# The last two tail-row results of an attention + MoE kernel: one 128-partition store each in place of two 64-partition stores

## The chip, the cores and the metric

The kernel runs on one core of a Trainium2 chip. The metric is device time in microseconds (us) of one execution, taken as the median of several runs. A profile is one more execution of the same program, recorded by the hardware; times inside it count from the first instruction of the span.

In what follows PE is the matrix engine, DVE the vector engine, ACT the scalar engine, POOL the GpSimd engine and SP the engine that does nothing but issue transfers and wait. A "q" behind a name (SPq, ACTq) is the instruction queue of that engine. All transfers run on the core's 16 DMA engines. Those that SP issues stand in the profile as queue q1, those that ACT issues as queue q10. A transfer is cut into packets, here one packet for each contiguous piece of memory, and closes with small 4-byte packets that raise its semaphore.

## The reference

Eight batches of eight heads of 576 tokens go through a linear attention with random features. The result is laid out as 4608 tokens x 512 and multiplied through a gated pair of weights:

```python
q_p, k_p = (phi(q_s), phi(k_s))
kv = np.einsum('bhsm,bhsd->bhmd', k_p, v)
z = np.sum(k_p, axis=2)
num = np.einsum('bhsm,bhmd->bhsd', q_p, kv)
den = np.einsum('bhsm,bhm->bhs', q_p, z)[..., None] + 1e-06
attn = num / den
x = attn.transpose(0, 2, 1, 3).reshape(B * S, H * D)      # 4608 x 512
a, b = x @ w_a, x @ w_b                                   # 4608 x 1536 each
return (a * b) @ w_out                                    # 4608 x 512, float32
```

## The kernel before

**Tiles of rows.** The 4608 rows of x are worked through in nine tiles of 512. Tiles 0 to 7 are the first 512 rows (`SM`) of each of the eight batches. The ninth tile, `b == B`, gathers the 64 tail rows (`TL`, rows 512 to 575) of all eight batches: 8 x 64 = 512 rows. It is the last work of the program. In it 128 partitions hold two batches: partitions 0 to 63 the tail rows of one batch (`j = 0`), partitions 64 to 127 those of the next (`j = 1`). A half `th` of the tile is four batches, which are two such groups of 128 rows, called t = 0 and 1 (or "parts").

**Order.** Every operation is recorded in a graph; a planner with costs, due times and tables of shifts lays out one order for all engines, and the program is emitted in that order. Each engine runs its own queue in that order and waits on semaphores. A transfer is an instruction in the queue of SP or of ACT, waits there for its data, is issued, and the engine goes on while the data moves.

**The output product.** The last two tiles use a scheme of seven block products (class `Out7`), so a result block of 256 rows x 256 columns is a sum of several PSUM banks and buffers in SBUF. Four buffers `oc` of 128 partitions x 2 parts x 256 columns hold the four blocks of the tile (half `th` of the rows, half `dh` of the columns). In the last tile, `second(q, dh)` (line 1267) makes the last product of a block, adds it to `oc` (`add`, line 1211, on DVE) and stores the block (`store`, line 1219). Three blocks are finished whole: one DVE addition of 128 x 512 and then the store. The fourth, (1, 1), the last of the program, is finished in two parts: for each t, the three matmuls of that part, a DVE addition of 128 x 256 (line 1213), and a store of that part.

**The stores of the last tile.** `rows` (line 1227) is the view of the output with axes j (2), r (64 rows of a batch), t and c (256 columns, 1 KB in a row). For each block or part, `store` issues two transfers: j = 0 on SP's queue, j = 1 on ACT's queue. So in the last tile there are three pairs of whole stores (64 rows x 2 parts x 1 KB, 128 KB each) and two pairs of part stores (64 rows x 1 KB, 64 KB each): ten transfers, five for each queue. Behind them SP waits for all transfers to land, and a closing sequence of all engines ends the program.

**Two other transfers that the prediction counts.** `zdr<-zx` writes 8 rows of 32 numbers (8 packets of 128 bytes). `xtd<-xts` writes 128 partitions x 4 pieces of 64 numbers (512 packets of 256 bytes). No other transfer has data packets under 512 bytes.

Of the kernel before, what the change touches and what calls it, by code (L numbers as in the profile page):

```python
# [18 lines left out]
P = 128  # L19
# [3 lines left out]
E, FF = H * D, 1536  # L23
# [3 lines left out]
HM = SM // 2  # L27
NFP = NF // 2
B1 = 2
TL = S - SM  # L30
# [352 lines left out]
def tile_attention_moe(ctx: ExitStack, tc: tile.TileContext, kqt, kqtt, kqn, kqnt, vx, omst, idn, wab, wout, out):  # L383
    nc = tc.nc
# [11 lines left out]
    g = Graph()  # L396
# [45 lines left out]
    def dma(dst, src):  # L442
        return lambda e: nc.sync.dma_start(dst(), src())
# [63 lines left out]
    for kind, i, ws in units:  # L507
# [27 lines left out]
        if kind == "o":  # L535
# [3 lines left out]
                 nbytes=P * 2 * E * 4)  # L539
# [630 lines left out]
    class Out7:  # L1170
# [48 lines left out]
        def store(self, o, th, dh, part=None):  # L1219

            b, cols = self.b, slice(HM * dh, HM * dh + HM)
            if b < B:
                r0 = b * S + HM * th
                g.op({"SP": 330}, dma(lambda: out[r0:r0 + HM, cols].rearrange("(t p) c -> p t c", p=P), lambda: o.ap[:]), r=[(o, None)], prio=-5,
                     nbytes=P * E * 4)
                return
            rows = out.rearrange("(n s) c -> n s c", s=S)[4 * th:4 * th + 4, SM:S, cols].rearrange("(t j) r c -> j r t c", j=2)
            tt = slice(0, 2) if part is None else slice(part, part + 1)
            for j, (eng, queue) in enumerate((("SP", nc.sync), ("ACT", nc.scalar))):
                g.op({eng: 330}, lambda e, j=j, queue=queue: queue.dma_start(rows[j][:, tt], o.ap[TL * j:TL * j + TL, tt]),  # L1230
                     r=[(o, part)], prio=-5, nbytes=TL * E * (4 if part is None else 2))

        def items(self, i, C, ghl, Sg, wo, ot):

# [288 lines left out]
    for b in range(B + 1):  # L1523
        if b < B1:
            moe_block(b)
        else:
            if b == B:

                for hp in range(NHP):
# [3 lines left out]
                         prio=-20, nbytes=P * SM * 4, deps=[steps[NF * (B - 1) + CFG["XL"][0]]])  # L1533
# [88 lines left out]
```

## Time and profile before

| | us |
|---|---|
| median of 3 runs | 1020.82 |
| lowest and highest of them | 1020.35, 1022.02 |
| the profiled execution's own time | 1018.96 |
| its span, first to last instruction | 1017.2 |
| PE busy in the span | 1006.6 (99%) |
| granted TensorE clock, mean of the span | 0.999 |

The profiled execution is 1.76 us longer than its span, and 1.86 us shorter than the median of the runs. The page gives busy times by engine, the span in 40 slices, the DMA queues and the chain of work that ended last; queries of the trace give rows by line, by window of time and by queue. The rows below were read from them. A window "A:B" is in us from the span's start.

### The profile page before, as it was taken

To read this page: it belongs to the slowest core of one execution; us is meant where nothing else is said; L and a number is where in the kernel's file an instruction comes from. 1 tells how busy PE (TensorE), PEld (TensorE's weight loads), DVE (VectorE), ACT (ScalarE), POOL (GpSimd) and SP (SyncE) were. 2 spreads that over 40 slices of the span, in tenths; PEclk is the share of its full clock that TensorE was granted. 3 is DMA by queue.
4 is the path that set the end of the run, shared out by engine and by line. 5 is a ranking of instruction groups with operands and counts; after the bars stand their busy time and mean duration, and the time that the engine had idled before them with its cause. 6 is when DMAs were issued, how large, how long until landed. Compare 5 with 4: busy or idle time off the path is not lost.

```text
span 1017.2 us, 27457 instructions
## 1 busy us (share of the span) xinstructions
PE 1006.6 (99%) x10538; PEld 890.0 (87%) x10538; DVE 873.1 (86%) x2162; ACT 574.6 (56%) x1584; POOL 110.7 (11%) x157
## 2 busy tenths in 40 slices
PE   9999999999999999999999999999999999999998
PEld 7777777777888999889988988988998999999997
DVE  7999999899997989877896889888887578999776
ACT  7998797667755647655663656575554024232221
POOL 0131212100111111110210111111110000000000
PEclk9999999999999999999999999999999999999999
DMA  9777887898999999999899889988887889999991
GB/s 356 289 268 256 284 258 223 302 337 306 307 332 383 308 311 303 330 321 312 269 317 357 285 288 328 335 286 294 279 300 256 295 290 347 315 354 337 374 328 44
DMA packets 123428, 306.76 MB, mean 302 GB/s; under 512 B 17952, under 2 KB 41248, under 8 KB 123296
## 3 DMA queue, kind: packets, MB, share of 16 engines
q1 hardware_dynamic: 122416, 304.34, 86.6%
q8 instruction: 83, 1.36, 0.6%
q10 hardware_dynamic: 880, 0.66, 0.2%
q14 instruction: 49, 0.40, 0.1%
HBM read 249.60 MB, written 55.34 MB: 300 GB/s over the span
## 4 chain that ended last, share of the span: by engine, by line
PE 92%; DVE 5%; DMA 1%; ACT 1%; issue 1%; SPq 0%; DVEq 0%; ACTq 0%
PE p L1418 39%; PE o L1137 23%; PE pb L1327 6%; PE pa L1327 6%; PE o_P L1206 5%; PE pkv L918 3%; PE ppk L641 3%; PE p L641 2%; PE p L990 2%; DMA X<-in_kqt_dram 1%; PE p L1206 1%; DVE sm L667 1%; PE ppq L641 1%; DVE raw L490 1%; PE pm L990 1%
## 5 line engine op out<-in xcount | busy, mean ns | idle before, releaser
L1428 DVE TENSOR_TENSOR c<-p,c 128x512 f32<-128x512 f32 (+1 forms) x336 | 208.0, 619 | 63.7 <-PE p L1418 60.7
L1137 PE MATMUL o<-wo,ghl 128*128 128x512 f32 x1008 | 255.9, 395 | 0.2 <-issue 0.2
L1137 PEld LDWEIGHTS o<-wo,ghl 128*128 128x128 f32 x1008 | 180.9, 188 | 38.5 <-issue 5.4
L1418 PE MATMUL p<-x,w 128*128 128x256 f32 x1008 | 136.2, 281 | 0.3 <-DVE c L1428 0.2
L1418 PEld LDWEIGHTS p<-x,w 128*128 128x128 f32 x1008 | 130.6, 189 | 6.6 <-DVE c L1428 0.9
L1418 PE MATMUL p<-Sa,t 128*128 128x256 f32 x1008 | 128.5, 276 | 0.0
L1418 PEld LDWEIGHTS p<-Sa,t 128*128 128x128 f32 x1008 | 121.0, 188 | 0.1
L432 ACT COPY c<-p 128x256 f32<-128x256 f32 x84 | 31.0, 369 | 115.1 <-PE p L1418 103.9
L948 ACT ACTIVATE hq<-hq,dn 128x128 f32<-128x128 f32 x224 | 69.7, 391 | 29.5 <-DVE dn L944 29.2
L865 POOL TENSOR_TENSOR z<-hk 128x256 f32<-128x256 f32 x28 | 25.2, 899 | 523.8 <-ACT hk L680 402.3
L1418 PE MATMUL p<-x,t 128*128 128x256 f32 x504 | 72.0, 278 | 0.8 <-DVE oc L1216 0.8
L938 DVE CUSTOM_DVE_ANT_0 zero<-hq,zb 128x128 bf16<-128x128 f32 x224 | 68.2, 304 | 4.1
L1418 PE MATMUL p<-Sb,bq 128*128 128x256 f32 x504 | 71.3, 277 | 0.0
L1418 PE MATMUL p<-Sb,t 128*128 128x256 f32 x504 | 71.0, 276 | 0.0
L680 ACT ACTIVATE hq<-hq,sm 128x128 f32<-128x128 f32 x196 | 64.7, 391 | 7.5 <-DVE sm L675 7.4
L1418 PEld LDWEIGHTS p<-x,t 128*128 128x128 f32 x504 | 64.8, 188 | 2.3 <-DVE oc L1216 1.0
L680 ACT ACTIVATE hk<-hk,sm 128x128 f32<-128x128 f32 x188 | 61.2, 391 | 8.2 <-DVE sm L675 8.1
L1418 PEld LDWEIGHTS p<-Sb,bq 128*128 128x128 f32 x504 | 63.9, 188 | 0.1
L1418 PEld LDWEIGHTS p<-Sb,t 128*128 128x128 f32 x504 | 63.6, 188 | 0.0
L432 ACT CAST ghl<-c 128x512 fp32r<-128x512 f32 (+1 forms) x60 | 32.8, 566 | 44.2 <-PE o L1137 25.8
L440 DVE TENSOR_TENSOR ghl<-c,ghl 128x512 fp32r<-128x512 f32 (+1 forms) x86 | 54.0, 641 | 4.2 <-ACT ghl L432 3.5
L1478 DVE TENSOR_TENSOR c<-c,c 128x512 f32<-128x512 f32 x82 | 55.5, 711 | 0.7
(245 smaller groups left out, 1898.4 us busy)
## 6 DMA issues: line engine op xcount, KB each, us to landing
t<-td SPq DMA_DIRECT2D x168, 512.0 KB
wo<-wod SPq DMA_DIRECT2D x96, 512.0 KB
bq<-bd SPq DMA_DIRECT2D x84, 256.0 KB
qdr<-qd SPq DMA_DIRECT2D x112, 144.0 KB
hq<-qdr SPq DMA_DIRECT2D x28, 576.0 KB
X<-in_kqt_dram SPq DMA_DIRECT2D x30, 512.0 KB
td<-ts SPq DMA_DIRECT2D x24, 512.0 KB
v<-in_vx_dram SPq DMA_DIRECT2D x28, 288.0 KB
```

Of the source, the lines that this page charges most:

```text
L432: nc.scalar.copy(o(), i())
L440: return lambda e: ENG[e].tensor_tensor(o(), i(), f(hi()), op=ALU.subtract)
L641: nc.tensor.matmul(flat4(pps[w])[half, c * M:c * M + M], x()[rows, c * P:c * P + P][:, half], om.ap[rows], start=True, stop=True)
L680: g.op({"ACT": 393 if b >= B1 or not own else 359}, lambda e, c=c, w=w, to=to, at=at: nc.scalar.activation(to.ap[:, at + c], src[w](c), AF ...
L938: g.op({"DVE": 302}, lambda e, c=c, qc=qc: nc.vector.tensor_tensor_reduce(out=junk.ap[:], in0=qc(), in1=zb.ap[:], scale=1.0, scalar=0.0, o ...
L948: g.op({"ACT": 392}, lambda e, c=c, src=src: nc.scalar.activation(hq.ap[:, c], src(), AF.Copy, scale=dn.ap[:, c:c + 1]), r=[sd, (dn, None) ...
L1137: nc.tensor.matmul(po.ap[:], ghl.ap[:, gi, t * P:(t + 1) * P], wo.ap[:, wi], start=(n == 0 and i == 0), stop=(n == NF - 1 and i == 2))
L1206: nc.tensor.matmul(pb.ap[:, t], A[0](ai)[:, t * P:(t + 1) * P], W[0](wi), start=begin and t == j == 0, stop=stop and t == 1 and j == 2)
L1327: nc.tensor.matmul(pb.ap[:], wt.ap[:, wi, c], xs[c].at(xi), start=(c == 0 and i == 0), stop=(c == NC4 - 1 and i == 2))
L1418: nc.tensor.matmul(pb.ap[:, half], wcol(wi, c), xc(xi, c), start=n == 0, stop=n == 5)
L1428: g.op({"DVE": dve(n)}, lambda e: nc.vector.tensor_tensor(c4.ap[:, o], pb.ap[:, half], y(), op=ALU.add), r=[*((pb, k) for k in range(half. ...
L1478: g.op({"DVE": dve(SM)}, lambda e, v=v, C=C: nc.vector.tensor_tensor(v(C[1]), v(C[1]), v(C[0]), op=ALU.mult), r=part, w=part[2:], prio=-10)
```

## The change

For a part store (`part is not None`) the loop over the two 64-partition halves is gone. One transfer takes all 128 partitions of the part: part 0 is issued on SP's queue and part 1 on ACT's queue. The whole stores are unchanged. Bytes, order of work and buffers are unchanged.

```diff
             rows = out.rearrange("(n s) c -> n s c", s=S)[4 * th:4 * th + 4, SM:S, cols].rearrange("(t j) r c -> j r t c", j=2)
             tt = slice(0, 2) if part is None else slice(part, part + 1)
-            for j, (eng, queue) in enumerate((("SP", nc.sync), ("ACT", nc.scalar))):
+            queues = ("SP", nc.sync), ("ACT", nc.scalar)
+            if part is not None:
+                eng, queue = queues[part]
+                g.op({eng: 330}, lambda e: queue.dma_start(rows[:, :, tt], o.ap[:, tt]),
+                     r=[(o, part)], prio=-5, nbytes=P * HM * 4)
+                return
+            for j, (eng, queue) in enumerate(queues):
                 g.op({eng: 330}, lambda e, j=j, queue=queue: queue.dma_start(rows[j][:, tt], o.ap[TL * j:TL * j + TL, tt]),
-                     r=[(o, part)], prio=-5, nbytes=TL * E * (4 if part is None else 2))
+                     r=[(o, part)], prio=-5, nbytes=TL * E * 4)
```

The order on PE, DVE and POOL is the same in both kernels. The end of SP's queue, with the dimensions of each transfer's pattern in the output behind its name (`oc_0` to `oc_3` are the four blocks, the branch is the end of the program):

```order
-L1230 DMA out_dram<-oc_0_13599 64x2x256
-L1230 DMA out_dram<-oc_1_14444 64x2x256
-L1230 DMA out_dram<-oc_2_14452 64x2x256
-L1230 DMA out_dram<-oc_3_14467 64x256 x2
-L1617 UNCONDITIONAL_BRANCH
+L1236 DMA out_dram<-oc_0_13599 64x2x256
+L1236 DMA out_dram<-oc_1_14444 64x2x256
+L1236 DMA out_dram<-oc_2_14452 64x2x256
+L1232 DMA out_dram<-oc_3_14467 2x64x256
+L1623 UNCONDITIONAL_BRANCH
```

The last two transfers of 64 x 256 have become one of 2 x 64 x 256. The end of ACT's queue, of the kernel before and of the changed one:

```order
L432 CAST ghl_10_14392<-c_51_14355 128x256
L1230 DMA out_dram<-oc_0_13599 64x2x256
L1230 DMA out_dram<-oc_1_14444 64x2x256
L1230 DMA out_dram<-oc_2_14452 64x2x256
L1230 DMA out_dram<-oc_3_14467 64x256 x2
L1617 UNCONDITIONAL_BRANCH
```

```order
L432 CAST ghl_10_14392<-c_51_14355 128x256
L1236 DMA out_dram<-oc_0_13599 64x2x256
L1236 DMA out_dram<-oc_1_14444 64x2x256
L1236 DMA out_dram<-oc_2_14452 64x2x256
L1232 DMA out_dram<-oc_3_14467 2x64x256
L1623 UNCONDITIONAL_BRANCH
```

ACT's queue changes in the same way. The leading dimension of the pattern in the output is the pair j (2), since the two 64-row halves belong to two batches that lie 576 rows apart; on the SBUF side the pattern leads with 128 partitions.

## Rows read from the trace of the kernel before

**Rows 1.** The page: busy time of each engine, share of the span, instructions.

```profile
PE 1006.6 (99%) x10538; PEld 890.0 (87%) x10538; DVE 873.1 (86%) x2162; ACT 574.6 (56%) x1584; POOL 110.7 (11%) x157
```

**Rows 2.** Chain of work that ended last, from 1010: start us, us, what.

```profile
1009.95 1.56 PE o_P L1206 x13
1011.51 0.73 PE p L1206 x6
1012.24 0.02 issue
1012.26 0.42 DVE oc L1213
1012.69 0.33 DVEq L1617
```

**Rows 3.** Timeline: last DVE additions; issues on SP and ACT: start us, us.

```profile
1012.60 0.41 DVE L1213 TENSOR_TENSOR oc<-p,oc 128x256 f32<-128x256 f32 x1
1010.11 0.68 SPq L1230 DMA_DIRECT2D out_dram<-oc  x1
...
1012.26 0.60 SPq L1230 DMA_DIRECT2D out_dram<-oc  x1
1012.27 0.63 ACTq L1230 DMA_DIRECT2D out_dram<-oc  x1
1012.96 0.57 SPq L1230 DMA_DIRECT2D out_dram<-oc  x1
1013.00 0.81 ACTq L1230 DMA_DIRECT2D out_dram<-oc  x1
1013.62 0.55 SPq L1230 DMA_DIRECT2D out_dram<-oc  x1
1013.90 0.55 ACTq L1230 DMA_DIRECT2D out_dram<-oc  x1
```

**Rows 4.** Waits of SP's queue, 1009 to 1018: us in total, times, longest.

```profile
SPq L1617 <- DMA out_dram<-oc: 1.9, 2, 1.7
```

**Rows 5.** DMA queues, window 1009:1018: busy tenths in 40 slices, packets, share.

```profile
DMA  0003000000088999997479899988720000000000
DMA packets 1185, 1.07 MB, mean 118 GB/s; under 512 B 160, under 2 KB 1184, under 8 KB 1184
q1 hardware_dynamic: 592, 0.52, 22.4%
q10 hardware_dynamic: 592, 0.52, 18.5%
```

**Rows 6.** Whole span: packets, and four of 36 rows of transfers issued.

```profile
DMA packets 123428, 306.76 MB, mean 302 GB/s; under 512 B 17952, under 2 KB 41248, under 8 KB 123296
t<-td SPq DMA_DIRECT2D x168, 512.0 KB
...
xtd<-xts SPq DMA_DIRECT2D x8, 128.0 KB
...
zdr<-zx SPq DMA_DIRECT2D x28, 1.0 KB
...
ident<-in_idn_dram ACTq DMA_DIRECT2D x1, 64.0 KB
```

**Rows 7.** Three windows: busy us by engine, PE clock, DMA share, GB/s.

```profile
1012.20:1012.60 0.40, 0.02 (x1) 0.00 (x0) 0.37 (x2) 0.00 (x0) 0.00 (x0) 1.00 1.08 377
1014.20:1014.60 0.40, 0.00 (x0) 0.00 (x0) 0.00 (x0) 0.00 (x0) 0.00 (x0) 1.00 1.02 328
930.00:940.00 10.00, 10.00 (x89) 10.00 (x88) 9.72 (x21) 3.31 (x8) 0.00 (x0) 1.00 1.03 410
```

**Rows 8.** DMA packets, windows 1010.5:1011.4, 1011.2:1011.5 and 1013.54:1014.15, its q10.

```profile
DMA packets 0, 0.00 MB, mean 0 GB/s; under 512 B 0, under 2 KB 0, under 8 KB 0
DMA packets 8, 0.01 MB, mean 27 GB/s; under 512 B 0, under 2 KB 8, under 8 KB 8
q10 hardware_dynamic: 1, 0.00, 0.1%
```

**Rows 9.** DMA queues, windows 1014.3:1014.53 and 1014.53:1014.63: q1; 1015.7:1016.2: all.

```profile
q1 hardware_dynamic: 6, 0.00, 3.0%
q1 hardware_dynamic: 11, 0.01, 31.6%
DMA packets 2, 0.00 MB, mean 0 GB/s; under 512 B 2, under 2 KB 2, under 8 KB 2
```

## The prediction

> **What bounds the kernel now.** I read the page first. PE is busy 99% of the span [rows 1], and the change touches no instruction of PE, DVE or POOL, so nothing before the last stores can move. What counts is the end, and there I read the chain of work that ended last, then the issues of transfers, then the packets. The chain leaves PE at 1012.24 and goes over the last DVE additions [rows 2]. The second part's addition starts at 1012.60 and takes 0.41, so the last result stands in SBUF at 1013.01 [rows 3]. The span ends at 1017.2. Between the two lies only the storing: SP waits 1.9 us for transfers into the output [rows 4], and the DMA engines are busy until about 1015.7 [rows 5]; behind 1015.7 only two closing packets of 4 bytes are left [rows 9]. So the program's last 4.2 us are transfers and the closing sequence, about 1.5 us of it (1017.2 - 1015.7) after the last data packet. What ends the data later or sooner by some time moves the end of the program by that time.
>
> **The transfers that go and come.** Four part stores of 64 rows go: SP issues its two at 1012.96 and 1013.62, ACT its two at 1013.00 and 1013.90 [rows 3]. Two of 128 rows come. SP's still starts at 1012.96, since SP's queue is busy with the whole store before it (1012.26 + 0.60) and not with waiting. ACT's waits for the second addition, 1013.01, so it starts at about 1013.05. The last issue so starts 0.85 us earlier (1013.90 to 1013.05). The gain is bounded by that 0.85 us if the packets behind it keep up.
>
> **What the packets do.** The ten transfers of the window move 1024 packets of 1 KB and close with 160 small packets [rows 5]: 16 for each transfer, so each of them, of 64 or 128 rows, ran on all 16 DMA engines. That isn't so of every transfer in this program. The 36 rows of issues add up to 866 transfers, and 16 closing packets for each would be 13,856. The span has 17,952 packets under 512 bytes [rows 6]; 8 x 512 = 4096 are data of xtd and 28 x 8 = 224 data of zdr, which leaves 13,632 that close a transfer. That is 224 short of 13,856, and 224 is 28 x 8: the 28 transfers of 8 rows close with 8 packets instead of 16. They ran on 8 engines. So how many engines a transfer gets follows from a dimension of its pattern. All others here lead with 32, 64, 128 or 256 on both sides and got 16. The new stores lead with 2 in the output and with 128 partitions in SBUF, a form that this trace doesn't have.
>
> Two readings fit the rows: the number of engines follows the leading dimension, and then a new store runs on 2 engines with 64 rows each; or it follows the number of rows in all, and then it runs on 16 with 8 rows each. In zdr both are 8, so the rows don't settle it. I give the first reading 0.84. The 2 x 64 rows of the output aren't one even run of 128: the two batches lie 576 rows apart, so the leading 2 can't be folded into the 64, and who splits such a pattern into equal shares without counting through it splits at the outermost level. That 128 rows stand on the SBUF side speaks for the second reading, 0.16.
>
> The Trainium skill ("DMA: Bandwidth & Descriptors", section "Why a DMA increments its semaphore by 16 and not by 1") states the first reading: the slowest dimension that isn't 1 is looked at on both sides, and the largest number up to 16 that divides both is the number of engines; here that is 2. It also says that the lowest-numbered ones are taken, so that both stores would share the same two. The 8 closing packets of zdr agree with it; no run so far shows the 2.
>
> **The sum on two engines.** How long one engine takes for a row of 1 KB is read where all 16 are full. At 377 GB/s an engine moves 23.6 GB/s, a row in 43.5 ns; at 328 GB/s it is 50 ns [rows 7]. Where rows are 4 KB the rate is 410 GB/s, 40 ns for each KB [rows 7]; that is the quick end. I take 44 ns, since the first window is full of 1 KB stores of this very kind. Both new stores have the pattern 2 x 64 on their queues and so, I take it, the same two engines: 128 rows on each, 128 x 44 ns = 5.6 us (5.1 at 40 ns, 6.4 at 50 ns). On 16 engines the same 256 rows are 16 x 44 = 0.7 us.
>
> They start where the part stores' packets start now. From the first whole store's issue (1010.11) to its first packet it is 1.3 us: none by 1011.4, 8 in the window to 1011.5 [rows 8]. That puts the early end at 1012.96 + 1.3 = 1014.25. In the trace SP's queue moves almost nothing from 1014.3 to 1014.53, while ACT's whole store drains, and 11 packets in the next 0.1 us [rows 9]; so 1014.55 is the late end. I take 1014.5, as the whole stores are kept. The data then ends at 1014.5 + 5.6 = 1020.1 against 1015.7, which is 4.4 us later (from 1014.25 + 5.1 - 1015.7 = 3.65 to 1014.55 + 6.4 - 1015.7 = 5.25). The issue that is 0.85 us earlier gives nothing back, as the two engines have rows of the first store until 1014.5 + 64 x 0.044 = 1017.3. The closing sequence behind it, 1.5 us, is kept. Two issues less on SP and ACT lie under the packets and are worth nothing.
>
> Against the profiled execution: span 1017.2 + 4.4 = 1021.6, its time 1018.96 + 4.4 = 1023.4. The median of the runs is 1.86 us above that execution, and a stretch added at the end is added to every run: 1020.82 + 4.4 = 1025.2.
>
> The page's figure for one engine, some 27 GiB/s ("DMA: Bandwidth & Descriptors", "Specifications"), would be 35 ns for a row; by it, as an estimate, the stores take 4.5 us and the median is 1024.1. No window here shows that rate.
>
> **The rivals.**
>
> *Sixteen engines.* If the engines are counted by rows in all, or if the pattern is regrouped on its way to the queue so that the change's leading 2 disappears, nothing is confined. Then the end looks like two pairs of whole stores, which the trace has: the pairs issued from 1010.11 on are through at 1013.55, where the last packet of ACT's queue stands [rows 8]; that is 3.44 us. The third pair starts at 1012.26 [rows 3], so the data ends at 1015.70, as now. Time 1020.8, from 1020.0 (all of the 0.85 us) upwards. For it: both sides carry 128 rows, and 64 x 2 patterns had 16 closing packets. Against it: the leading dimension was 64 there. This is the case that ends not slower. It decides from four engines upwards: with four, a shared engine has 64 rows, 64 x 44 ns = 2.8 us, 1.6 us later than now (1014.5 + 2.8 - 1015.7), which is under 2.04.
>
> The skill's section "Rules for kernel authors" on the same page advises one transfer of 128 partitions in place of two of disjoint halves, since both halves run on the same 16 engines. By that rule alone this rival would hold; the trace agrees that each half ran on 16, but the rule speaks of halves that one plain pattern can join, and another row of the same table warns of an outermost dimension under 16.
>
> *Two engines for each store, but not the same two.* Then the stores run side by side: 64 x 44 ns = 2.8 us, the later from about 1014.6, so the data ends at 1017.4, 1.7 us later: 1022.5. The two queues ran over the same 16 engines at once [rows 5, 7], so I see no reason why one pattern should get two different pairs; little speaks for it. It is within 0.2% of before. The point from which the outcome turns to slower is 2.04 us of added packets: more than about 80 rows on the fullest engine behind 1014.5 (1017.74 - 1014.5 = 3.2 us at 40 to 44 ns).
>
> **How the numbers follow.** A difference under 0.2%, 2.04 us, counts as no change. Two engines hold 0.84 (above); that both stores get the same two I put at 19 in 20 of that, 0.8, at 1025.2. Its own range, with the spread of the runs (1020.35 to 1022.02) on the two bounds: 1020.35 + 3.65 = 1024.0 to 1022.02 + 5.25 = 1027.3. Two separate engines: 0.04, 1022.5. Sixteen engines: 0.16, 1020.8. The first case's range holds a little under 0.8 for itself, so the range given reaches down to the second case: 1022.3 to 1027.3. Slower by over 0.2%: 0.81. Within: 0.17 (the rival with sixteen engines, and most of the second). Faster by over 0.2%: 0.02, since not even the 0.85 us of issue comes near 2.04.
>
> **What would show it.** Right: in the last 10 us of the changed kernel the DMA engines are busy at two sixteenths (about 0.12) for some 5 us; the small packets are 6 x 16 + 2 x 2 = 100 instead of 160; SP's wait for the output grows from 1.7 to about 6 us; PE, DVE and all before 1012 are the same. Wrong: 128 small packets (8 x 16) and a DMA share near 1 up to the end, which is the first rival; 100 small packets and four engines busy (share about 0.25) for some 3 us is the second. If a lone engine moves a row in much more or less than 44 ns, the step that fails is the price of a row, and the time moves by 0.13 us for each ns.

## The result and the profile after

The changed kernel takes 1027.2 us (median of 6 runs, 1025.62 to 1029.04), the kernel before 1021.27 us (median of 6, 1020.35 to 1023.2). The ratio is 1.0057, with a 95% interval of 1.0043 to 1.0072: it is slower by 5.9 us of median (4.4 to 7.4 by the interval). The profiled execution took 1026.78 us, its span is 1025.0 us against 1017.2.

All of what the change costs stands behind the last DVE addition. The page's first rows and the chain show that nothing else moved: as many instructions on each engine, the same pieces of PE and DVE work at the end as in [rows 2], 2.41 us later on the clock.

```profile
PE 1007.7 (98%) x10538; PEld 890.3 (87%) x10538; DVE 875.6 (85%) x2162; ACT 575.0 (56%) x1584; POOL 110.9 (11%) x157
```

The end of the chain of work that ended last (start us, us, what) in the changed kernel:

```profile
1013.92 0.73 PE p L1206 x6
1014.65 0.02 issue
1014.67 0.42 DVE oc L1213
1015.10 0.33 DVEq L1623
```

So the two spans differ by 7.8 us, and two things are in that. One is the run itself: the first whole store of the last tile is issued at 1010.11 in [rows 3] and at 1012.52 here. In the profiles of all other kernels below that have this issue, and whose code up to there is the same, that point lies between 1012.03 and 1013.31. Runs of the kernel before alone spread from 1019.91 to 1024.49 in a later series of 13, and the profiled execution of before, with 1018.96 us, is quicker than any of them. The other is the tail, counted from that issue on SP to the end of the span: **7.1 us before (1017.2 - 1010.11), 12.5 us after (1025.0 - 1012.52), 5.4 us more.** From that issue to the end of the last addition it is 2.9 us in every kernel that has it, before included (1013.01 - 1010.11), so the tail leaves out how quickly a run got there. The experiments are read by it; each tail is that of one profiled execution.

The first whole store's issue and the last issues on SP and ACT in the changed kernel (start us, us), which answer to [rows 3]:

```profile
1012.52 0.68 SPq L1236 DMA_DIRECT2D out_dram<-oc  x1
...
1014.68 0.60 SPq L1236 DMA_DIRECT2D out_dram<-oc  x1
1015.37 0.58 SPq L1232 DMA_DIRECT2D out_dram<-oc  x1
...
1015.46 1.31 ACTq L1232 DMA_DIRECT2D out_dram<-oc  x1
```

ACT's last issue starts 2.94 us after the first whole store, where it was 3.79 before (1013.90 - 1010.11): the 0.85 us are there, as counted. What they are worth shows in the packets from 1009 to 1026, in 40 slices (busy tenths of all 16 DMA engines, GB/s, packets), beside [rows 5]:

```profile
DMA  0000000100049998799101111111111111000000
GB/s 0 0 0 0 0 0 0 39 0 0 0 108 198 371 321 212 166 176 287 22 12 29 39 48 43 34 48 48 48 48 48 48 48 46 19 0 0 0 0 0
DMA packets 1125, 1.07 MB, mean 63 GB/s; under 512 B 100, under 2 KB 1124, under 8 KB 1124
```

The whole stores run at up to 371 GB/s with the engines 7 to 9 tenths busy. Then, for some 6.5 us, the busy share is 1 tenth; the rate moves between 12 and 48 GB/s in the first 3 us of it and then stays at 48 until shortly before the end. The small packets are 100 instead of 160: six transfers that close with 16 and two that close with 2. In the windows below (busy us by engine, then PE clock, DMA share and GB/s at the end of each line) the share is about two sixteenths (0.125) all the way until the last rows, and only the rate changes:

```profile
1017.20:1017.80 0.60, 0.00 (x0) 0.00 (x0) 0.00 (x0) 0.00 (x0) 0.00 (x0) 0.99 0.11 10
1017.80:1018.40 0.60, 0.00 (x0) 0.00 (x0) 0.00 (x0) 0.00 (x0) 0.00 (x0) 0.50 0.13 29
1018.40:1019.00 0.60, 0.00 (x0) 0.00 (x0) 0.00 (x0) 0.00 (x0) 0.00 (x0) 0.50 0.12 43
1019.00:1020.00 1.00, 0.00 (x0) 0.00 (x0) 0.00 (x0) 0.00 (x0) 0.00 (x0) 0.50 0.13 40
1020.00:1021.00 1.00, 0.00 (x0) 0.00 (x0) 0.00 (x0) 0.00 (x0) 0.00 (x0) 0.50 0.14 48
...
1023.00:1023.80 0.80, 0.00 (x0) 0.00 (x0) 0.00 (x0) 0.00 (x0) 0.00 (x0) 0.50 0.10 36
```

Both queues share these two engines. In the window 1020:1021.5 both have packets in flight (packets, MB, share of 16 engines), and together they have the 48 GB/s that ACT's queue alone has in 1022:1023, which the last two lines show:

```profile
DMA packets 71, 0.07 MB, mean 48 GB/s; under 512 B 0, under 2 KB 71, under 8 KB 71
q1 hardware_dynamic: 40, 0.04, 7.7%
q10 hardware_dynamic: 31, 0.03, 5.9%
...
DMA packets 47, 0.05 MB, mean 48 GB/s; under 512 B 0, under 2 KB 47, under 8 KB 47
q10 hardware_dynamic: 47, 0.05, 13.5%
```

In the slow stretch the two engines don't stand idle; their rows take longer. In the window 1017.3:1018.3 SP's queue moves this:

```profile
q1 hardware_dynamic: 18, 0.02, 12.6%
```

That is 0.112 us of an engine for each row (0.126 x 16 x 1.0 us / 18), where in 1020:1021.5 it is 0.046 (0.077 x 16 x 1.5 us / 40).

SP waits for all of these rows at the end, where [rows 4] had 1.9 us (us in total, times, longest):

```profile
SPq L1623 <- DMA out_dram<-oc: 8.0, 4, 4.3
```

### The profile page after: what moved, and what is told of

It reads as the page before. It is cut to its first block, busy times and chain, and to the rows that moved or that the text cites. A ratio compares the mean times of both kernels' runs of the same rounds, so it can differ in the third digit from the quotient of the medians.

```text
span 1025.0 us, 27453 instructions
## 1 busy us (share of the span) xinstructions
PE 1007.7 (98%) x10538; PEld 890.3 (87%) x10538; DVE 875.6 (85%) x2162; ACT 575.0 (56%) x1584; POOL 110.9 (11%) x157
## 4 chain that ended last, share of the span: by engine, by line
PE 83%; DVE 9%; DMA 3%; ACT 3%; issue 1%; SPq 0%; DVEq 0%; ACTq 0%
PE p L1424 37%; PE o L1137 21%; PE o_P L1206 5%; PE pb L1333 4%; PE pa L1333 4%; PE pkv L918 3%; PE ppk L641 2%; PE p L641 2%; PE p L990 2%; DMA X<-in_kqt_dram 1%; DVE sm L667 1%; DVE raw L490 1%; PE p L1206 1%; DMA wo<-wod 1%; PE ppq L641 1%
```

## The experiments

The theory: the leading dimension of the output's pattern, 2, confines each new store to two engines, and it is the same two for both. Its rivals: one store of 128 rows on a queue is slow whatever its pattern; the distance of the two batches in DRAM is what is slow; each store had two engines of its own. Edits are against the changed kernel, and " ..." marks lines left out between two places. "Scratch" is a buffer in DRAM that nothing reads. Each tail is the span minus the time of the first whole store's issue on SP, both as the profile prints them.

### Two groups of 64 rows that lie close together

```diff
+    scr = [dram.tile([2, P // 2 + 8, HM], F32, name=f"scr{t}") for t in range(2)]
 ...
-                g.op({eng: 330}, lambda e: queue.dma_start(rows[:, :, tt], o.ap[:, tt]),
+                g.op({eng: 330}, lambda e: queue.dma_start(scr[part][:, :P // 2], o.ap[:, part]),
```

> The two part stores go to a scratch buffer in DRAM whose pattern is 2 x 64 rows as in the changed kernel, but with the two groups 72 rows apart instead of 576 (8 rows of padding); the last block's rows are missing in the output. Measure: the tail, from the issue of the first whole store on SP to the end of the span: 7.09 us before, 12.48 us in the changed kernel. Leading dimension sets the engines: 2 engines, 128 rows on each, tail 12.0 to 12.8 us, 100 small packets in the last window. Distance of the two batches in DRAM is what is slow: tail about 7 us.

Measured: tail 12.4 us (1025.5 - 1013.11), 100 small packets in the window 1013:1025.6:

```profile
DMA packets 1124, 1.05 MB, mean 83 GB/s; under 512 B 100, under 2 KB 1124, under 8 KB 1124
```

With the groups 72 rows apart the tail is as long as with 576, so the distance of the batches isn't what is slow.

### Four groups of 32 rows

```diff
+    scr = [dram.tile([4, P // 4 + 8, HM], F32, name=f"scr{t}") for t in range(2)]
 ...
-                g.op({eng: 330}, lambda e: queue.dma_start(rows[:, :, tt], o.ap[:, tt]),
+                g.op({eng: 330}, lambda e: queue.dma_start(scr[part][:, :P // 4], o.ap[:, part]),
```

> As the near 2 x 64 scratch store, but with the pattern 4 x 32 rows (padded so that it cannot be joined). Leading dimension sets the engines: 4 engines, 64 rows on each, 64 x 42 ns = 2.7 us of packets, tail 8.6 to 9.2 us, 104 small packets. Any single 128-row store on a queue is slow whatever its pattern: tail about 12.5 us. Number of rows in all sets the engines: tail about 7, 128 small packets.

Measured: tail 10.0 us (1022.2 - 1012.21). The packets of the window 1012.1:1022.3, in slices of 0.255 us:

```profile
DMA  0000018899978698994111222222222110000000
GB/s 0 0 0 0 0 44 209 189 313 386 361 225 213 149 213 157 233 349 64 12 36 52 60 72 80 96 96 96 96 92 72 56 44 24 20 0 0 0 0 0
DMA packets 1128, 1.05 MB, mean 103 GB/s; under 512 B 104, under 2 KB 1128, under 8 KB 1128
```

104 small packets: each store closed with 4. The plateau is 96 GB/s, twice the 48 of two engines. So four engines, as the theory has it. The time doesn't fit: the expected tail was 8.6 to 9.2. The row shows where. The rate climbs for six slices before it reaches 96 and falls for six behind it, and the whole lasts 4.1 us (16 slices) where 64 rows at 42 ns are 2.7. Windows of it tell the climb from the fall:

```profile
1017.00:1017.50 0.50, 0.00 (x0) 0.00 (x0) 0.00 (x0) 0.00 (x0) 0.00 (x0) 0.50 0.20 29
1017.50:1018.00 0.50, 0.00 (x0) 0.00 (x0) 0.00 (x0) 0.00 (x0) 0.00 (x0) 0.50 0.24 57
...
1020.50:1021.00 0.50, 0.00 (x0) 0.00 (x0) 0.00 (x0) 0.00 (x0) 0.00 (x0) 0.50 0.07 23
```

In the climb the share is near four sixteenths (0.20 and 0.24 of 0.25) at a low rate: the engines are busy and their rows are slow. Behind the plateau the share falls, to 0.07 in the last of these windows, so the engines end at different times. The part of the expectation that failed is the size of this start, for which it had no term, not the count of engines.

### Sixteen groups of 8 rows, and one plain pattern of 128 rows

```diff
+    scr = [dram.tile([16, P // 16 + 8, HM], F32, name=f"scr{t}") for t in range(2)]
 ...
-                g.op({eng: 330}, lambda e: queue.dma_start(rows[:, :, tt], o.ap[:, tt]),
+                g.op({eng: 330}, lambda e: queue.dma_start(scr[part][:, :P // 16], o.ap[:, part]),
```

> As before with the pattern 16 x 8 rows. Leading dimension sets the engines: 16 engines, 16 rows on each, 0.7 us of packets, tail 6.8 to 7.2 us, 128 small packets. Any single 128-row store is slow: tail about 12.5 us. A pattern of several levels is slow: tail well over 8 us.

```diff
+    scr = [dram.tile([P, HM], F32, name=f"scr{t}") for t in range(2)]
 ...
-                g.op({eng: 330}, lambda e: queue.dma_start(rows[:, :, tt], o.ap[:, tt]),
+                g.op({eng: 330}, lambda e: queue.dma_start(scr[part], o.ap[:, part]),
```

> As before with one plain pattern of 128 rows in the scratch buffer. Leading dimension sets the engines: as 16 x 8, tail 6.8 to 7.2 us, 128 small packets; it also shows what the idea of one 128-partition store would be worth at best against the 7.09 us of before. Any single 128-row store is slow: about 12.5 us.

Measured: tail 6.7 us with 16 x 8 (1019.4 - 1012.66) and 6.8 us with the plain pattern (1019.0 - 1012.20). The window 1012.5:1019.5 of 16 x 8, which is full to the end:

```profile
DMA  0000000018999999788659989999999510000000
GB/s 0 0 0 0 0 0 0 0 53 211 199 193 281 380 375 392 234 240 222 176 141 228 176 164 252 357 275 258 275 363 328 193 29 0 0 0 0 0 0 0
DMA packets 1152, 1.05 MB, mean 150 GB/s; under 512 B 128, under 2 KB 1152, under 8 KB 1152
```

One store of 128 rows for each part is not slow in itself, nor is a pattern of several levels. Nor is it the scratch buffer that makes these two quick, since two groups of 64 rows went to one too and were slow. With 16 engines the tail is even 0.3 to 0.4 us shorter than that of the four stores of before, as far as one profile of each can tell; the 16 x 8 tail lies a little under the 6.8 that was expected. That is all that the idea had to give.

### Eight groups of 16 rows

```diff
+    scr = [dram.tile([8, P // 8 + 8, HM], F32, name=f"scr{t}") for t in range(2)]
 ...
-                g.op({eng: 330}, lambda e: queue.dma_start(rows[:, :, tt], o.ap[:, tt]),
+                g.op({eng: 330}, lambda e: queue.dma_start(scr[part][:, :P // 8], o.ap[:, part]),
```

> The part stores go to a scratch buffer as 8 x 16 rows (padded); the last block's rows are missing in the output. Leading dimension sets the engines: 8 engines, 32 rows on each, 1.35 us of packets; with 2, 4 and 16 measured at 12.44, 9.95 and 6.77 us of tail, and the slow first rows growing with the rows on an engine, 7.3 to 8.4 us; 112 small packets.

Measured: tail 7.8 us (1021.1 - 1013.31), 112 small packets in the window 1013.2:1021.2:

```profile
DMA packets 1136, 1.05 MB, mean 131 GB/s; under 512 B 112, under 2 KB 1136, under 8 KB 1136
```

With it the row is complete: leading 2, 4, 8 and 16 give tails of 12.4, 10.0, 7.8 and 6.7 us, and 100, 104, 112 and 128 small packets.

### One of the two new stores alone

Part 0 keeps its two stores of 64 rows, part 1 is one store of 2 x 64.

```diff
-            if part is not None:
+            if part == 1:
                 eng, queue = queues[part]
 ...
-                     r=[(o, part)], prio=-5, nbytes=TL * E * 4)
+                     r=[(o, part)], prio=-5, nbytes=TL * E * (4 if part is None else 2))
```

> Only part 1 is stored as one transfer of 2 x 64 rows (on ACT); part 0 keeps its two transfers of 64 rows. Tail from the issue of the first whole store on SP to the end of the span: 7.06 us before, 12.47 us changed. Both stores share the same two engines in the changed kernel, so that one alone has half the rows on each: 64 x 42 ns = 2.7 us instead of 5.4; with the slow first rows of about 1.2 us tail 9.5 to 10.4 us, without them 8.7 to 9.2; 130 small packets (8 x 16 + 2). The two stores had two engines each: the tail stays at about 12.

Measured: tail 9.9 us (1022.3 - 1012.39), 130 small packets in the window 1012.3:1022.4:

```profile
DMA packets 1154, 1.05 MB, mean 104 GB/s; under 512 B 130, under 2 KB 1154, under 8 KB 1154
```

Half the rows on the two engines take 2.6 us off the 12.5. Two engines for each store would have left the tail at about 12; that rival falls, as the 48 GB/s of both queues together had said.

### The two new stores with nothing before them

```diff
+            if part is None:
+                return
             queues = ("SP", nc.sync), ("ACT", nc.scalar)
```

> The three whole stores of the last tile are left out (their rows are missing in the output); the two part stores of 2 x 64 rows are kept as in the changed kernel, alone on the DMA engines. It asks where the slow first rows come from: in the changed kernel 6.6 us pass from the first row of the part stores to the last, though 128 rows at 42 ns are 5.4. If the rows of the whole stores before them were in the way, the two stores now take 5.4 to 5.7 us from first row to last. If it lies in how the rows of such a transfer are handed to two engines, again 6.4 to 6.8 us. The 16-engine share stays at 2 of 16.

Measured: the stores' data lasts from 1013.9 to 1020.7, 6.8 us, with 260 packets in all (256 rows, 4 that close). Windows of it:

```profile
1013.90:1014.40 0.50, 0.00 (x0) 0.00 (x0) 0.00 (x0) 0.00 (x0) 0.00 (x0) 1.00 0.12 25
...
1015.40:1015.90 0.50, 0.00 (x0) 0.00 (x0) 0.00 (x0) 0.00 (x0) 0.00 (x0) 1.00 0.10 23
1015.90:1016.40 0.50, 0.00 (x0) 0.00 (x0) 0.00 (x0) 0.00 (x0) 0.00 (x0) 1.00 0.14 49
1016.40:1016.90 0.50, 0.00 (x0) 0.00 (x0) 0.00 (x0) 0.00 (x0) 0.00 (x0) 0.96 0.12 16
1016.90:1017.40 0.50, 0.00 (x0) 0.00 (x0) 0.00 (x0) 0.00 (x0) 0.00 (x0) 0.50 0.12 25
...
1018.00:1019.00 1.00, 0.00 (x0) 0.00 (x0) 0.00 (x0) 0.00 (x0) 0.00 (x0) 0.50 0.14 49
```

The slow start is still there though no whole store precedes: 25 GB/s in the first half microsecond, 23 from 1015.4, 49 from 1015.9, again 16 and 25 from 1016.4 to 1017.4, and 49 later. So the whole stores' rows are not in the way; the start belongs to the confined transfers themselves. The second dip comes with the first rows of ACT's store. By queue, the window 1016.4:1017.4 has:

```profile
q10 hardware_dynamic: 10, 0.01, 9.5%
q1 hardware_dynamic: 10, 0.01, 2.9%
```

Ten rows of the store that begins take 0.152 us of an engine each (0.095 x 16 x 1.0 us / 10), and in the same microsecond ten rows of the store that is under way take 0.046. So the slow rows are the first ones of a store, not those of engines that are slow as such.

### The same rows in four transfers of 2 x 32

```diff
+    scr = [[dram.tile([2, P // 4 + 8, HM], F32, name=f"scr{t}{h}") for h in range(2)] for t in range(2)]
 ...
-                g.op({eng: 330}, lambda e: queue.dma_start(rows[:, :, tt], o.ap[:, tt]),
-                     r=[(o, part)], prio=-5, nbytes=P * HM * 4)
+                for h in range(2):
+                    g.op({eng: 330}, lambda e, h=h: queue.dma_start(scr[part][h][:, :P // 4], o.ap[TL * h:TL * h + TL, part]),
+                         r=[(o, part)], prio=-5, nbytes=TL * HM * 4)
```

> Each part goes to scratch buffers as two transfers of 2 x 32 rows (64 partitions each) on the same queue, so four transfers instead of two, with the same 128 rows on each of two engines; the last block's rows are missing in the output. It asks what the time beyond 128 x 42 ns belongs to: 1.2 us in the changed kernel, 0.85 us where one such transfer stood alone. If each transfer pays it at its start (0.6 to 0.85 us), last row 0.6 to 1.7 us later than in the changed kernel and tail 13.0 to 14.2 us. If it goes with the number of rows handed to an engine, tail 12.3 to 12.6 us as before. 104 small packets (6 x 16 + 4 x 2).

Measured: tail 12.3 us (1024.6 - 1012.29), 104 small packets in the window 1012.3:1024.7:

```profile
DMA packets 1128, 1.05 MB, mean 85 GB/s; under 512 B 104, under 2 KB 1128, under 8 KB 1128
```

Twice as many transfers pay no more in all, so it isn't a fixed price of each transfer. That it goes with the rows handed to an engine fits this run, but 2 x 64 and 4 x 32 lose about as much (1.2 and 1.4 us), though an engine has half the rows in the second. What makes the start slow stays open.

### The last block stored like the other three

Two transfers of 64 partitions x 2 parts, after both additions.

```diff
                             self.add(o, pb, o, part=t)
-                            self.store(o, q, dh, t)
+                        self.store(o, q, dh)
```

> The last block is still added in two parts, but stored like the other three: two transfers of 64 partitions x 2 parts, so as many transfers and rows in each as in the changed kernel, and a pattern that leads with 64. Leading dimension sets the engines: 16 engines, tail 6.7 to 7.1 us, 128 small packets, median within 0.2% of before (1021 us). A store of 128 rows or two issues instead of four is what costs: tail about 12 us, 1026 to 1027.

Measured: tail 6.7 us (1018.7 - 1012.03), 128 small packets, median 1020.64 us (10 runs, 1020.21 to 1021.82) against 1021.69 us of before (13 runs), ratio of the fast runs 0.9993 with an interval of 0.9983 to 1.0003. It issues as few transfers as the changed kernel, each of as many rows, and writes all of the output; it differs from it in what leads the pattern, and in that both wait for the second addition. Its window 1011.9:1018.8:

```profile
DMA  0000000028899999898648998999969900000000
DMA packets 1152, 1.05 MB, mean 152 GB/s; under 512 B 128, under 2 KB 1152, under 8 KB 1152
```

The tail is 0.4 us shorter than in the one profile of before. By time it can't be told from before, so it isn't shown to beat it.

## Why the prediction was right, and where its sizes were off

**What bounds the end.** Right. Nothing on PE or DVE moved but by the spread of runs, and the change is seen in the tail alone.

**The number of engines.** Right, and this decided the sign. The prediction drew it from a count over 866 transfers in which those of 8 rows closed with 8 packets, and from there had to choose between leading dimension and rows in all. The runs settle the choice: with 128 rows throughout, leading 2, 4, 8 and 16 close with 2, 4, 8 and 16 packets. The Trainium skill ("DMA: Bandwidth & Descriptors", section "Why a DMA increments its semaphore by 16 and not by 1") had the rule, and the packets of all eleven kernels agree with it. The other rule weighed, from the section "Rules for kernel authors" on the same page of the Trainium skill, to use one 128-partition transfer for two halves, did no harm where the joined pattern still spreads over 16 engines (tails 6.7 to 6.8 against 7.1 us), and fails here.

**The same two engines.** Right: 48 GB/s for both queues together, and 2.6 us less when one of the two stores is split as before. Which of the sixteen they are, no trace here tells.

**The size.** The prediction had 4.4 us later data and the median at 1025.2; the tail grew by 5.4 and the median by 5.9, to 1027.2, just under the upper end of the range (1027.3). That it lies inside is in part luck: the upper bound was made of rows of 50 ns and of the spread of the runs, and the largest part of what filled it was a slow start that no term allowed for. By the prediction's own steps:

- A row of 1 KB was put at 44 ns. At 48 GB/s one of two engines moves 24 GB/s, 42.7 ns a row: 128 rows take 5.5 instead of 5.6 us, 0.1 less. This term was right.
- The start was put 4.4 us behind the first whole store's issue (1014.5 - 1010.11). The confined rows start at 1017.2 (the slice with 10 GB/s), 4.7 behind: 0.3 more.
- **The mis-sized term is the time on two engines.** The prediction let the two engines run at full rate from the first row. Between 1017.2 and 1018.4 they moved at 10 and then 29 GB/s instead of 48, and lost again (40) when the second store began. 256 rows took 6.6 us (1017.2 to 1023.8) instead of 5.5: 1.1 more, since the first rows held an engine longer (0.112 us each in 1017.3:1018.3). No row of before shows it, since every transfer there that is near the end had 16 engines.
- The closing sequence was put at 1.5 us; from 1023.8 to 1025.0 it is 1.2: 0.3 less.

4.4 - 0.1 + 0.3 + 1.1 - 0.3 = 5.4. The rest of the median's 5.9 lies within the spread of the runs. Of the 2.0 us between 1025.2 and 1027.2, these steps are 1.0; another 0.45 is that the median of before came out at 1021.27 of six runs, where the prediction had 1020.82 of three.

**What was to show it.** Two sixteenths of DMA share and 100 small packets: as said, though for 6.6 us and not for some 5. "SP's wait for the output grows from 1.7 to about 6 us" was off: the longest single wait grew from 1.7 to 4.3 us, and all of them together from 1.9 to 8.0. The 0.85 us of earlier issue was counted as worth nothing while the two engines have work; it is there in the issues and doesn't show in the tail. Where 16 engines carry the stores, the tail is 0.3 to 0.4 us shorter.

**The rivals.** Sixteen engines at 1020.8 did not come, but the kernels that have them (16 x 8, plain 128, by half) have tails of 6.7 to 6.8 against 7.1, so its price of about nothing was right. The price of four engines was not: the prediction put them 1.6 us later than before and so within its 2.04 us of no change, and 4 x 32 rows measured 2.9 us (10.0 - 7.1). It is the same mis-sized term, and it didn't touch the outcome.

## What to carry to other kernels

Before two transfers are joined into one, look at the leading dimension of the joined pattern on both sides, not at its partitions or bytes: with 2, 4 or 8 in front in DRAM, a transfer of 128 rows ran on that many DMA engines here. (The SBUF side led with 64 or 128 in all these runs; a small one there was not tried.) Count the small packets that close transfers (16 for each is the healthy number) and read the DMA share of the last stretch; both tell it from the profile alone. At the end of a program, where nothing covers a transfer, a saved issue was worth tenths of a microsecond at most here, and a confined transfer costs the rows on one engine times its row time (42.7 ns for 1 KB here), and a slow start on top (1.1 to 1.4 us here with two and four engines).

## What the runs showed of the hardware

- A transfer confined to few engines doesn't start at their full rate. On two engines the first 1.2 us ran at 10 and 29 GB/s before 48; without other stores before it, the first half microsecond ran at 25. On four engines the climb to 96 GB/s took some 1.5 us, and the engines ended at different times. In that time the engines are busy, and it is the first rows of a store that take long: 0.11 and 0.15 us of an engine each, against 0.046 later. Four transfers of 2 x 32 rows had no more of it in all than two of 2 x 64. Its cause wasn't found.
- ACT's issue of the second store took 1.31 us on two engines, 1.32 on four and 1.38 on eight, where it took 0.76 us with 16 x 8 and 0.75 with the plain pattern. SP's issue of the first took 0.56 to 0.65 us in all of these. The row of the changed kernel stands above; that of 16 x 8 is this:

```profile
1015.60 0.76 ACTq L1233 DMA_DIRECT2D scr<-oc  x1
```

- The profiled execution of one and the same body reached the same point of the program anywhere from 1010.11 to 1013.31. A change at the end that is worth a few tenths of a microsecond is read from the tail, not from the span.
